# Soft-MoE dispatch softmax taken with a running maximum in two groups of chunks

## Chip, cores and metric

One core of a Trainium2 chip runs the whole program. The metric is device time in microseconds, the median of three runs. Engines are named as in the profile: PE is TensorE (PEld its weight loads), DVE VectorE, ACT ScalarE, POOL GpSimd, SP SyncE, whose queue issues nearly all transfers.

## What is computed

A two-dimensional Fourier transform of x (8 x 3072 x 256), of which the real part is kept, gives 24576 tokens of 256 numbers. A soft mixture of experts follows: 32 slots, dispatched by a softmax over all tokens, eight small experts, and a combining softmax over the slots. Then a feed-forward layer with a squared ReLU. Cut to what matters:

```python
X = np.fft.fft(np.fft.fft(x, axis=1), axis=2).real.reshape(24576, 256)
logits = X @ phi
d = np.exp(logits - logits.max(0, keepdims=True))
d /= d.sum(0, keepdims=True) + 1e-09
slot_input = d.T @ X
# experts: slot_out = relu(slot_input @ w1[e]) @ w2[e]
c = softmax of logits over the 32 slots
y = c @ slot_out
out = (s * np.maximum(y @ w_in, 0.0) ** 2 + b) @ w_out
```

The maximum in the third line runs over all 24576 tokens, one number for each of the 32 slots.

## The kernel before

The transform is never formed. phi is turned by the small transform along the 256 features first (phd), x is multiplied with it, and the long transform is done on 32 columns in place of 256. The stages, in the order of time:

- To about 90 us: x is read in 24 pages of 1 MiB, projected and partly transformed into `tt`.
- **Logits** (lines 553 to 611): 16 chunks `lp` of 112 partitions x 512, two at a time, each by eight small products. ScalarE copies a chunk to `lg` in SBUF, VectorE reduces it to 32 maxima in `cm` (L585). The two don't read one chunk at the same time: one is told to wait for the other. Behind the last chunk comes the maximum over all (L592), a transpose (L598), one reduction more (L603), a product that spreads the 32 numbers over all partitions (L607), and the copy `cmb`. Warm-up products of ones (`keep_warm`, L190) stand between on PE. Two VectorE steps of the preparation of w_out (L216, `side_step`) and six small ACT copies (`fill_stack`) lie in this gap too.
- **Transform of the exponentials** (L614 to L670, tiles `dt`, `hp`, `hh`): for each chunk the maximum is subtracted (POOL for odd chunks, DVE for even, L633), ACT takes the exponential (L669), PE makes four products with a table (`hp`, L652; the profile shows each as two), and ACT and DVE copy one half each to `hh` (L643). The four `dt` buffers are a pool of their own.
- **Sums** (L695 to L745, `htp`, `dps`, `racc`): `hh` is transposed, transformed once more and multiplied with the 24 pages `xrt` of x, which gives slot_input. Beside it DVE, POOL and ACT make the combining softmax (`c_steps`) and DVE prepares w_in and w_out (`side_step`, three steps in each round from the sixth on).
- **Experts** with w1 and w2, then the feed-forward part from about 232 us to the end.

The order on each engine is that in which the code is written; nothing reorders it. All large operands live in pages of 1 MiB (`page`, `drop`): 15 in `ring`, later some in smaller pools that take freed memory. The list `todo` holds the loads that are still to come in a fixed order: the 24 pages xrt, four pages of w_in among them, eight of w1, eight of w2. `pump()` issues the next as soon as the program has dropped a page, and SP waits at that load until the last reader of the page is done, with all later loads behind it.

Of the kernel before, what the change touches and what calls it, by code (L numbers as in the profile page):

```python
# [8 lines left out]
F32 = mybir.dt.float32  # L9
# [23 lines left out]
def tile_fft2__then__softmoe__then__act_relu2(  # L33
# [492 lines left out]
    cmb = keep.tile([P, NE], F32, name="cmb")  # L526
# [25 lines left out]
    temps = tc.alloc_tile_pool(name="temps", bufs=1, side="right")  # L552
    cm = temps.tile([R, NCH + 1, NE], F32, name="cm")
    cm1 = temps.tile([R, NE], F32, name="cm1")
    def lgf(i):
        return lg[i // 4][:, 4 * (i % 4):4 * (i % 4) + 4].rearrange("p k g e -> p (k g) e")

    with tc.tile_pool(name="ps_l", bufs=6, space=PSUM) as psl, \
            tc.tile_pool(name="ps_m", bufs=1, space=PSUM) as psm:
        mxp[:] = [psm, 1]  # L560
        done_l = 0
        for st in range(NCH // 2 + SKEW):
            halves = [(h, st - SKEW * h) for h in range(2) if 0 <= st - SKEW * h < NCH // 2]
            lps = {h: psl.tile([R, KC, NG * NE], F32, name="lp") for h, _ in halves}
            for k in range(2 * KC):
                q = P // 2 * (k % 2)
                m = M if q else P // 2
                for h, i8 in halves:
                    r = slice(64 * h, 64 * h + 64)
                    nc.tensor.matmul(  # L570
                        lps[h][q:q + m, k // 2, :], lhsT=ltabs[i8 // 4][0][r, 2 * KC * (i8 % 4) + k, 0:m],
                        rhs=tt[r, 2 * KC * i8 + k].rearrange("p b e -> p (b e)"), start=True, stop=True,
                        tile_position=(64 * h, q), skip_group_check=True,
                    )
            for h, i8 in halves:
                if h and i8 % 4 == 3:
                    drop(ltabs[i8 // 4][1])
                lp = lps[h]
                busy("dve", 0.55)
                at["pe"] += 1.06  # L580
                dst = lg[i8 // 2][:, 8 * (i8 % 2) + h:8 * (i8 % 2) + 8:2].rearrange("p k g e -> p k (g e)")
# [6 lines left out]
                if done_l == NCH - 4:  # L588
                    nc.vector.tensor_reduce(out=cm[:, NCH, :], in_=cm[:, :NCH - 4, :].rearrange("p i e -> p e i"), axis=AX.X,
                                            op=ALU.max)  # L590
                if done_l == NCH - 1:
                    nc.vector.tensor_reduce(out=cm1, in_=cm[:, NCH - 4:, :].rearrange("p i e -> p e i"), axis=AX.X,  # L592
                                            op=ALU.max)
                done_l += 1
        warm = psl.tile([R, 2, B * NE], F32, name="lp")[:, 0, :R]
        keep_warm(warm, 8)
# [3 lines left out]
        while side_step(0.0, True):  # L600
            pass
# [18 lines left out]
    def lgc(i):  # L620
        return lg[i // 4][:, 4 * (i % 4):4 * (i % 4) + 4]
# [688 lines left out]
```

## Time and profile before

| | |
|---|---|
| median of three runs | 1399.73 us (1397.64 to 1401.19) |
| span of the profiled execution | 1411.6 us |
| PE busy | 1388.2 us, 98% |
| DVE, ACT, POOL busy | 83%, 72%, 17% |
| chain that ended last, by engine | PE 88%, DMA 2%, DVE 1% |

The page gives the profiled execution's span and no other time of it. PE counts as busy while a product is in flight, so 98% does not say that it runs at its peak. The granted clock of PE has two levels, 2.4 GHz (shown as 1.00) and 1.2 GHz (0.50). The feed-forward part makes up five sixths of the span; the change lies in the stretch from 90 to 142 us.

### The profile page before, as it was taken

The page shows a single profiled execution, that of the slowest core. Times are in us where ns is not written, and L with a number is a line of the kernel's source. Part 1 is how long each engine was busy: PE and PEld are TensorE (multiplying, and loading weights), DVE is VectorE, ACT ScalarE, POOL GpSimd, SP SyncE. Part 2 cuts the span into 40 slices and gives each one's busy share as a digit, 9 for nine tenths or more (in the row PEclk, how much of TensorE's full clock was granted, in tenths as well). Part 3 has the DMA queues.
Part 4 walks back from the last instruction along what each step waited for, and adds up shares of the span by engine and source line. Part 5 has one row for each costly group of instructions (what it writes and reads, how often), then busy time and mean ns, then how long its engine had stood idle before and what let it go on. Part 6 is the DMA issues. An engine that isn't in the chain of part 4 may idle for free.

```text
span 1411.6 us, 23102 instructions
## 1 busy us (share of the span) xinstructions
PE 1388.2 (98%) x9036; PEld 856.0 (61%) x9036; DVE 1171.9 (83%) x1490; ACT 1010.7 (72%) x1423; POOL 233.1 (17%) x287
## 2 busy tenths in 40 slices
PE   8989999999999999999999999999999999999998
PEld 5669564566666666666666666666666666666665
DVE  1565764998989999999989898989898989888886
ACT  2774314877777777777877787877777777777775
POOL 1143400021212121211112121111111111111110
PEclk9995999999999999999999999999999999999999
DMA  8995795101010101101010101010101010101001
GB/s 352 414 311 229 291 414 225 29 27 36 20 36 23 36 24 29 30 23 32 23 36 21 34 23 36 23 33 23 36 23 36 23 36 23 33 23 36 23 20 30
DMA packets 72381, 112.27 MB, mean 80 GB/s; under 512 B 33904, under 2 KB 59632, under 8 KB 64976
## 3 DMA queue, kind: packets, MB, share of 16 engines
q1 hardware_dynamic: 72144, 110.70, 23.1%
q8 instruction: 71, 1.16, 0.3%
q14 instruction: 38, 0.31, 0.1%
q0 software_dynamic: 128, 0.10, 0.0%
HBM read 78.48 MB, written 25.17 MB: 73 GB/s over the span
## 4 chain that ended last, share of the span: by engine, by line
PE 88%; DMA 2%; DVE 1%; issue 1%; SPq 0%; ACT 0%; POOL 0%; DVEq 0%; ACTq 0%; POOLq 0%
PE op L1151 46%; PE op L1154 23%; PE fhp L1121 12%; PE racc L727 3%; DMA w2t<-in_moe_w_dram 2%; PE hp L652 2%; PE dps L712 1%; PE lp L570 1%; SPq L1084 0%; DVE cm L585 0%; DVE r L1127 0%; DVE rhl L1112 0%; PE eop L957 0%; DMA g<-gs 0%; PE gp L1055 0%
## 5 line engine op out<-in xcount | busy, mean ns | idle before, releaser
L1151 PE MATMUL op<-whl,rhl 128*128 128x512 f16 x3072 | 1025.3, 379 | 0.8 <-ACT rhl L1111 0.6
L1154 PE MATMUL op<-whl,rhl 128*128 128x256 f16 x3072 | 835.7, 273 | 0.0
L1126 ACT ACTIVATE r<-fhp,wsc 128x768 f32<-128x768 f32 (+1 forms) x513 | 461.8, 900 | 230.0 <-PE fhp L1121 228.8
L1127 DVE SCALAR_TENSOR_TENSOR r<-fhp,r 128x768 f32<-128x768 f32 (+1 forms) x513 | 488.9, 953 | 113.6 <-ACT r L1126 104.0
L1112 DVE TENSOR_TENSOR rhl<-r,rhl 128x768 f16<-128x768 f32 x511 | 506.9, 992 | 0.9 <-ACT rhl L1111 0.9
L1151 PEld LDWEIGHTS <-rhl 128*128 128x128 f16 x3072 | 300.5, 98 | 335.4 <-ACT rhl L1111 0.9
L1111 ACT CAST rhl<-r 128x768 f16<-128x768 f32 x511 | 420.1, 822 | 1.8 <-DVE r L1127 1.8
L1154 PEld LDWEIGHTS <-rhl 128*128 128x128 f16 x3072 | 300.6, 98 | 62.7 <-issue 0.3
L1166 POOL TENSOR_TENSOR ot<-ot,bias 128x256 f32<-128x256 f32 x189 | 138.1, 731 | 974.2 <-DVE ot L1164 974.2
L1121 PE MATMUL fhp<-ct,g 128*128 128x384 f16 x1024 | 250.4, 326 | 1.1 <-DMA g<-gs 0.8
L1121 PEld LDWEIGHTS <-g 128*128 128x128 f16 x1024 | 99.9, 98 | 69.0 <-issue 1.1
L1163 ACT ACTIVATE o<-op,small 128x256 f32<-128x256 f32 x189 | 90.0, 477 | 16.7 <-PE op L1154 16.7
L1164 DVE SCALAR_TENSOR_TENSOR ot<-op,small,o 128x256 f32<-128x256 f32 x192 | 91.7, 478 | 0.3
L394 PE MATMUL vt<-xb,phd 128*64 128x384 f32 (+3 forms) x288 | 49.0, 477 | 5.3 <-DMA xb<-in_x_turned_dram 5.3
L727 PE MATMUL racc<-xrt,dh 128*64 128x256 f32 x384 | 44.5, 383 | 0.4 <-DVE dh L717 0.4
L394 PEld LDWEIGHTS vt<-xb,phd 128*64 128x64 f32 x288 | 26.5, 139 | 25.5 <-issue 13.8
L727 PEld LDWEIGHTS racc<-xrt,dh 128*64 128x64 f32 x384 | 26.3, 137 | 20.9 <-issue 4.5
L419 DVE COPY v<-vq 128x512 f32<-128x512 f32 (+1 forms) x15 | 8.3, 593 | 33.9 <-PE vq L415 33.9
L406 ACT COPY vts<-vt 128x512 f32<-128x512 f32 (+1 forms) x16 | 8.5, 533 | 32.1 <-PE vt L394 32.0
L464 ACT COPY tt<-tps 32x512 f32<-32x512 f32 x48 | 27.7, 577 | 4.9 <-PE tps L450 4.4
L652 PE MATMUL hp<-htab_t,dt 112*128 112x104 f32 x128 | 27.6, 422 | 0.2 <-ACT dt L669 0.2
L652 PEld LDWEIGHTS hp<-htab_t,dt 112*128 112x128 f32 x128 | 27.4, 333 | 0.5 <-issue 0.5
(229 smaller groups left out, 518.0 us busy)
## 6 DMA issues: line engine op xcount, KB each, us to landing
xb<-in_x_turned_dram SPq DMA_DIRECT2D x24, 1024.0 KB, 20.1
xrt<-in_x_pages_dram SPq DMA_DIRECT2D x24, 1024.0 KB, 13.9
out_dram<-ot SPq DMA_DIRECT2D x128, 128.0 KB, 1.7
w1t<-in_moe_w_dram SPq DMA_DIRECT2D x8, 1024.0 KB, 13.7
out_dram<-ot SPq DMA_DIRECT2D x128, 64.0 KB, 2.0
raw<-in_moe_w_out_dram SPq DMA_DIRECT2D x4, 1024.0 KB, 20.3
raw<-in_moe_w_in_dram SPq DMA_DIRECT2D x4, 1024.0 KB, 7.8
w2t<-in_moe_w_dram SPq DMA_DIRECT2D x4, 1024.0 KB, 17.8
```

What stands on the lines that cost most here:

```text
L652: nc.tensor.matmul(hp[q][:, k, :], start=True, stop=True, lhsT=dt.rearrange("p k g e -> p (k g e)")[:, 128 * (2 * k + q):128 * (2 * k + q) ...
L727: nc.tensor.matmul(raccs[acc][64 * h:64 * h + 64, :], lhsT=dh[:, m, g].rearrange("p j e -> p (j e)"), rhs=xr[k][0][:, g, t, :], start=(sum ...
L1111: nc.scalar.copy(a, r2)
L1112: nc.vector.tensor_tensor(out=l, in0=r2, in1=a, op=ALU.subtract)
L1121: nc.tensor.matmul(hp[k * split][:, k, :].rearrange("p (s b m) -> p s b m", s=2, b=B), lhsT=g16[:, f * P:(f + 1) * P], rhs=c, start=True, ...
L1126: nc.scalar.activation(out=r[:, k], in_=hp[i][:, k], func=AF.Relu, scale=wsc[:, 2, p:p + 1])
L1127: nc.vector.scalar_tensor_tensor(out=r2[:, k], in0=hp[i][:, k], scalar=0.0, in1=r[:, k], op0=ALU.max, op1=ALU.mult)
L1151: nc.tensor.matmul(op.rearrange("p h d -> p (h d)"), lhsT=a, rhs=w.rearrange("p h d -> p (h d)"), start=(f == 0), stop=False)
L1154: nc.tensor.matmul(op[:, 0, :], lhsT=l, rhs=w[:, 0, :], start=False, stop=(f == NFC - 1))
L1163: nc.scalar.activation(out=o1, in_=op[:, 1, :], func=AF.Copy, scale=qv)
L1164: nc.vector.scalar_tensor_tensor(out=ot, in0=op[:, 0, :], scalar=qv, in1=o1, op0=ALU.mult, op1=ALU.add)
L1166: nc.gpsimd.tensor_tensor(out=ot, in0=ot, in1=bias, op=ALU.add)
```

## The change

The column maximum is taken in two groups. The first group (chunks of the first three of eight steps, six chunks) gets its maximum `cmb[0]` while the other logits are still being made (`top(0, ...)`); its chunks are subtracted from on POOL and DVE with that maximum. Their exponentials and transform stand directly behind the last logits on PE. The maximum of all 16 chunks, `cmb[1]`, is found between the first transform products (`top(1, ...)`) and used for the other ten. What the first group lacks is one factor for each slot, exp of the difference of the two maxima (`fac`), which POOL multiplies into the first group's part of `hh` in two passes (in place, 128 x 52 x 24 numbers each). The warm-up products are gone from here, DVE reduces a chunk before ACT copies it, two chunks share an `hp` tile and are copied at once, and of the copies of the first half of `hh` every third pair goes to DVE. `fill_stack` moves behind the fourth chunk. The scratch for the exponentials (seven buffers) and `cm` are two pages (`scr`) held from before the logits to the end of the transform. The steps of w_out that lay in the gap stay on the list of side work and are done among the sums.

```diff
-    cmb = keep.tile([P, NE], F32, name="cmb")
+    cmb = [keep.tile([P, NE], F32, name=f"cmb{g}") for g in range(2)]
...
+    GA, ND = 3, 7
+    scr = [page([R, 4, KC, NG, NE], F32, "scr") for _ in range(2)]
...
+    cm = scr[1][0][:, 3].rearrange("p k g e -> p (k g) e")
+    tmp = tabp.tile([P, 16, NE], F32, tag="tab", name="tmp")
+    cmr = [tmp[0:R, g] for g in range(2)]
+    dg = [tmp[0:NE, 2 + g] for g in range(2)]
+    cm2 = tmp[0:NE, 4]
+    dfa, fac = tmp[0:NE, 5, 0:1], tmp[:, 6, 0:1]
+    rep = tmp[0:NE, 8:12]
+    nc.gpsimd.tensor_copy(rep, ident[:NE, :NE].unsqueeze(1).to_broadcast([NE, 4, NE]))
...
+    def emit_d(i):
+        dts[i] = scr[i % ND // 4][0][:, i % ND % 4]
+        (nc.gpsimd if i in (0, 1, 2, 3) or i > 4 and i % 2 else nc.vector).tensor_tensor(
+            out=dts[i].rearrange("p k g e -> p (k g) e"), op=ALU.subtract, in0=lgc(i).rearrange("p k g e -> p (k g) e"),
+            in1=cmb[i >= 2 * GA][:R].unsqueeze(1).to_broadcast([R, 16, NE]),
+        )
+    def emit_exp(i):
+        for h in [slice(0, 2), slice(2, 4)] if i == 0 else [slice(0, 4)]:
+            nc.scalar.activation(out=dts[i][:, h], in_=dts[i][:, h], func=AF.Exp)
...
+    def top(g, step):
+        if step == 0:
+            nc.vector.tensor_reduce(out=cmr[g], in_=cm[:, 0:NCH if g else 2 * GA].rearrange("p i e -> p e i"), axis=AX.X, op=ALU.max)
+        elif step == 1:
+            top_t.append(psm.tile([P, P], F32, tag="tps", name="mt")[0:NE, 0:R])
+            nc.tensor.transpose(top_t[g], cmr[g], ident[:R, :R])
+        elif step == 2:
+            nc.vector.tensor_reduce(out=cm2[:, g:g + 1], in_=top_t[g], axis=AX.X, op=ALU.max)
+            nc.vector.tensor_scalar(out=dg[g], in0=ident[:NE, :NE], scalar1=cm2[:, g:g + 1], scalar2=None, op0=ALU.mult)
+        elif step == 3:
+            top_b.append(psm.tile([P, P], F32, tag="tps", name="mb")[:, 0:NE])
+            nc.tensor.matmul(top_b[g], lhsT=ones[:NE, :], rhs=dg[g], start=True, stop=True)
+        else:
+            nc.vector.tensor_copy(cmb[g], top_b[g])
+            if g:
+                nc.vector.tensor_tensor(out=dfa, in0=cm2[:, 0:1], in1=cm2[:, 1:2], op=ALU.subtract)
...
-                if done_l < NCH - 1:
-                    nc.scalar.copy(dst, lp)
-                lv = lp.rearrange("p k (b e) -> p (k b) e", e=NE)
-                nc.vector.tensor_reduce(out=cm[:, done_l, :], in_=lv.rearrange("p k e -> p e k"), axis=AX.X, op=ALU.max)
-                if done_l == NCH - 1:
-                    nc.scalar.copy(dst, lp)
...
-        warm = psl.tile([R, 2, B * NE], F32, name="lp")[:, 0, :R]
-        keep_warm(warm, 8)
-        mt = psm.tile([NE, R], F32, tag="mt", name="mt")
-        nc.tensor.transpose(mt, cm1, ident[:R, :R])
-        keep_warm(warm, 3)
-        while side_step(0.0, True):
-            pass
...
-        nc.vector.tensor_copy(cmb, mb)
-        mxp[0] = None
-        keep_warm(warm, 8)
-        fill_stack()
...
+        if st == GA + 1:
+            top(0, 1)
+        if st == GA + 2:
+            top(0, 3)
...
+            nc.vector.tensor_reduce(out=cm[:, 2 * i8 + h, :], in_=lv.rearrange("p k e -> p e k"), axis=AX.X, op=ALU.max)
+            nc.scalar.copy(dst, lp)
+            if n == 0 and st == GA + 1:
+                top(0, 2)
+            if n == 0 and st == GA + 2:
+                top(0, 4)
+        if st == GA:
+            top(0, 0)
+        if st == GA + 2:
+            for i in range(4):
+                emit_d(i)
+    top(1, 0)
+    emit_exp(0)
+    emit_exp(1)
+    emit_d(4)
+    emit_d(5)
...
+        def h_out(i, n):
+            o = 4 * (i % 2)
             for q in range(2):
-                hpv = hps[i][q].rearrange("p k (q c m) -> p (k q) c m", q=2, c=2)
-                eng = nc.vector.tensor_copy if q else nc.scalar.copy
-                eng(hh[q].rearrange("p m (c k) -> p k c m", c=2)[:, KC * i:KC * i + KC], hpv)
-            hps.pop(i)
+                hpv = hps[i // 2][q].rearrange("p k (q c m) -> p (k q) c m", q=2, c=2)[:, o:o + 4 * n]
+                eng = nc.vector.tensor_copy if q or (n > 1 and i // 2 % 3 == 2) else nc.scalar.copy
+                eng(hh[q].rearrange("p m (c k) -> p k c m", c=2)[:, KC * i:KC * (i + n)], hpv)
...
+            if i < 2:
+                top(1, 2 * i + 1)
+                top(1, 2 * i + 2)
+            if i == 3:
+                fp = psm.tile([P, P], F32, tag="tps", name="fp")[:, 0:1]
+                nc.tensor.matmul(fp, lhsT=rep.rearrange("p r e -> p (r e)"), rhs=dfa, start=True, stop=True)
...
+            if i > NCH - 2:
+                h_out(i - 1, 1)
+            elif i > 0 and i % 2 == 0:
+                h_out(i - 2, 2)
+            if 5 < i + 5 < NCH:
+                emit_d(i + 5)
...
+            if i + 2 < NCH:
+                emit_exp(i + 2)
+            if i == 3:
+                nc.scalar.activation(out=fac, in_=fp, func=AF.Exp)
+                fill_stack()
+            if i in (7, 11):
+                hq = hh[i // 11].rearrange("p m (c k) -> p m c k", c=2)[:, :, :, 0:2 * KC * GA]
+                nc.gpsimd.tensor_scalar(out=hq, in0=hq, scalar1=fac, scalar2=None, op0=ALU.mult)
+    for _, k_ in scr:
+        drop(k_)
```

PE behind the last logits, before: warm-up products (`L190`), the transpose `mt` and the spreading product `mb` stand ahead of the first `hp` product.

```order
L570 MATMUL lp<-tt,ltab 64x128
L570 MATMUL lp<-tt,ltab 48x128
L190 MATMUL lp<-ones 112x112 x8
L598 MATMUL mt<-ident,cm_785 32x112
L190 MATMUL lp<-ones 112x112 x3
L607 MATMUL mb<-dg,ones 128x32
L190 MATMUL lp<-ones 112x112 x8
L652 MATMUL hp_1038<-htab_t,dt 128x104
```

The same place in the change:

```order
L610 MATMUL lp<-tt,ltab 64x128
L610 MATMUL lp<-tt,ltab 48x128
L666 MATMUL hp_998<-htab_t,scr 128x104
L666 MATMUL hp_999<-htab_t,scr 128x104
L666 MATMUL hp_998<-htab_t,scr 128x104
L666 MATMUL hp_999<-htab_t,scr 128x104
L588 MATMUL mt<-ident,tmp 32x112
L666 MATMUL hp_998<-htab_t,scr 128x104
```

The transform's products follow the logits, and the second maximum's transpose stands among them.

DVE from the last logits on, before (`L585` reduces a chunk, `L589` and `L592` the reductions, `L216` is the side work):

```order
L585 TENSOR_REDUCE cm<-lp 112x32 x13
L589 TENSOR_REDUCE cm<-cm 112x32
L585 TENSOR_REDUCE cm<-lp 112x32 x3
L592 TENSOR_REDUCE cm_785<-cm 112x32
L216 SCALAR_TENSOR_TENSOR whl<-wo,wsc,whl 128x2x256 x2
L603 TENSOR_REDUCE cm_986<-mt 32x1
L605 TENSOR_SCALAR dg<-ident,cm_986 32x32
L608 COPY cmb<-mb 128x32
```

In the change:

```order
L627 TENSOR_REDUCE scr<-lp 112x32 x7
L585 TENSOR_REDUCE tmp<-scr 112x32
L627 TENSOR_REDUCE scr<-lp 112x32
L590 TENSOR_REDUCE tmp<-mt 32x1
L591 TENSOR_SCALAR tmp<-ident,tmp 32x32
L627 TENSOR_REDUCE scr<-lp 112x32 x2
L596 COPY cmb_757<-mb 128x32
L627 TENSOR_REDUCE scr<-lp 112x32 x6
L585 TENSOR_REDUCE tmp<-scr 112x32
```

The first group's three short steps have moved in among the chunk reductions, `L589` and the side work are gone from here, and only the second group's reduction is left behind the last chunk.

SP around the end of the transform, before, with what each load waits for (a load of one of the 24 xrt pages; DMAHW is the landing of the eighth load before it, the engines are the readers of the page):

```order
L326 DMA xrt_1224<-in_x_pages_dram 128x2048 [waits DVE_49,DMAHW2_49,Activation_49,Pool_49]
L326 DMA xrt_1226<-in_x_pages_dram 128x2048 [waits DMAHW3_49,PE_49,Pool_49]
L326 DMA xrt_1228<-in_x_pages_dram 128x2048 [waits DMAHW4_49,PE_49,Pool_49]
L326 DMA xrt_1275<-in_x_pages_dram 128x2048 [waits DMAHW5_49,PE_49]
L326 DMA xrt_1324<-in_x_pages_dram 128x2048 [waits DMAHW6_49,PE_49]
```

In the change:

```order
L326 DMA xrt_1079<-in_x_pages_dram 128x2048 [waits DMAHW0_49,PE_49,Pool_49]
L326 DMA xrt_1159<-in_x_pages_dram 128x2048 [waits DMAHW1_49,PE_49,Pool_49]
L326 DMA xrt_1161<-in_x_pages_dram 128x2048 [waits DMAHW2_49,DVE_49,Activation_49]
L326 DMA xrt_1163<-in_x_pages_dram 128x2048 [waits DMAHW3_49,DVE_49,Activation_49]
L326 DMA xrt_1210<-in_x_pages_dram 128x2048 [waits DMAHW4_49,PE_49]
```

The second and third rows before wait for the two halves of the table `htab`, freed in the middle and at the end of the transform, and the fourth for the first sum: one load starts at the end of the stage. In the change the first row waits for the first half of the table; the next three for its second half and for the two scratch pages, all freed at the end of the stage; the last for the first sum. Ten of the 24 pages xrt stand ahead of the stage's end there, against thirteen.

## Rows read from the trace of the kernel before

**Rows 1.** Timeline of PE: start us, us, line, instruction, idle before it.
```profile
98.89 6.72 PE L570 MATMUL lp<-tt,ltab 64*48 64x128 f32 x132 [3.88 <-issue]
105.54 1.82 PE L190 MATMUL lp<-ones 128*112 128x112 f32 x16
108.61 0.27 PE L598 MATMUL mt<-ident,cm 112*32 112x112 f32 x1 [1.25 <-DVE cm L592]
...
110.44 0.63 PE L607 MATMUL mb<-dg,ones 32*128 32x32 f32 x2 [0.97 <-DVE dg L605]
```

**Rows 2.** Chain that ended last, in order of time: start us, us, what.
```profile
105.58 0.73 DVE cm L589
106.31 1.80 DVE cm L585 x3
108.14 0.42 DVE cm L592
108.56 1.32 DVE whl L216 x2
...
111.45 1.72 POOL dt L633
...
114.55 27.61 PE hp L652 x128
...
203.89 18.57 DMA w2t<-in_moe_w_dram
222.48 9.61 DMA w2t<-in_moe_w_dram
```

**Rows 3.** Table by stretch; its first row names the columns.
```profile
core 0: us, PE busy (x) PEld busy (x) DVE busy (x) ACT busy (x) POOL busy (x), PEclk, DMA share, GB/s
...
93.20:96.50 3.30, 1.64 (x46) 1.16 (x36) 3.30 (x6) 2.22 (x5) 2.98 (x5) 1.00 1.06 235
...
103.40:106.80 3.40, 3.40 (x66) 3.00 (x59) 3.08 (x5) 2.05 (x4) 0.00 (x0) 1.00 1.01 419
106.80:110.20 3.40, 1.43 (x13) 1.07 (x11) 3.26 (x8) 1.46 (x7) 0.00 (x0) 1.00 1.02 417
110.30:114.50 4.20, 3.89 (x18) 3.56 (x18) 2.65 (x4) 1.90 (x4) 3.05 (x2) 0.50 1.02 421
114.50:142.20 27.70, 27.65 (x130) 27.67 (x131) 10.96 (x22) 13.96 (x29) 7.97 (x7) 0.50 0.40 161
...
155.00:203.90 48.90, 48.90 (x397) 27.93 (x396) 37.24 (x49) 7.01 (x13) 5.91 (x6) 1.00 0.99 396
...
142.20:155.00 12.80, 12.15 (x105) 7.28 (x104) 10.22 (x21) 6.11 (x11) 8.74 (x9) 0.92 0.53 176
```

**Rows 4.** Timeline of ACT, where the logits resume.
```profile
100.36 1.07 ACT L583 COPY lg<-lp 112x512 f32<-112x512 f32 x2 [4.94 <-PE lp L570]
```

**Rows 5.** Instructions on tile lp: ns min/median/max, first and last start us.
```profile
L585 DVE TENSOR_REDUCE cm<-lp x16: 680/681/693, 92.2 to 107.4; 112x32 f32<-112x512 f32 x16
L583 ACT COPY lg<-lp x15: 586/591/632, 91.6 to 105.1; 112x512 f32<-112x512 f32 x15
```

**Rows 6.** Groups by line, 114 to 142.3 us: busy us, mean ns, idle before.
```profile
L633 POOL TENSOR_TENSOR dt<-lg,cmb 112x512 f32<-112x512 f32 x7 | 9.3, 1336 | 14.6 <-ACT hh L643 14.6
L669 ACT ACTIVATE dt<-dt 112x512 f32<-112x512 f32 x14 | 8.8, 627 | 0.0
L643 DVE COPY hh<-hp 128x208 f32<-128x208 f32 x16 | 8.4, 522 | 17.5 <-PE hp L652 17.5
L643 ACT COPY hh<-hp 128x208 f32<-128x208 f32 x16 | 8.2, 514 | 13.5 <-PE hp L652 13.5
```

**Rows 7.** Groups by line on POOL, 89 to 95 us, the same columns.
```profile
L513 POOL COPY ltab<-ltab 64x2048 f32<-64x2048 f32 x1 | 1.9, 1895 | 0.9 <-DMA ltab<-in_ltab_dram 0.9
```

**Rows 8.** Transfers, 142 to 235 us: queue, packets, MB, share of 16 engines.
```profile
q1 hardware_dynamic: 6352, 32.51, 88.8%
```

More of the change, by code (lines that the diff above doesn't have):

```diff
@@ new lines, in tile_fft2__then__softmoe__then__act_relu2 @@
+    top_t, top_b = [], []
+    psl = tc.alloc_tile_pool(name="ps_l", bufs=6, space=PSUM)
+    for st in range(NCH // 2 + SKEW):
+        halves = [(h, st - SKEW * h) for h in range(2) if 0 <= st - SKEW * h < NCH // 2]
+        lps = {h: psl.tile([R, KC, NG * NE], F32, name="lp") for h, _ in halves}
+        for k in range(2 * KC):
+            q = P // 2 * (k % 2)
+            m = M if q else P // 2
+            for h, i8 in halves:
+                r = slice(64 * h, 64 * h + 64)
+                nc.tensor.matmul(
+                    lps[h][q:q + m, k // 2, :], lhsT=ltabs[i8 // 4][0][r, 2 * KC * (i8 % 4) + k, 0:m],
+                    rhs=tt[r, 2 * KC * i8 + k].rearrange("p b e -> p (b e)"), start=True, stop=True,
+                    tile_position=(64 * h, q), skip_group_check=True,
+                )
+        if st == GA + 1:
+            top(0, 1)
+        if st == GA + 2:
+            top(0, 3)
+        for n, (h, i8) in enumerate(halves):
+            if h and i8 % 4 == 3:
+                drop(ltabs[i8 // 4][1])
+            lp = lps[h]
+            busy("dve", 0.55)
+            at["pe"] += 1.06
+            dst = lg[i8 // 2][:, 8 * (i8 % 2) + h:8 * (i8 % 2) + 8:2].rearrange("p k g e -> p k (g e)")
+            lv = lp.rearrange("p k (b e) -> p (k b) e", e=NE)
+            nc.vector.tensor_reduce(out=cm[:, 2 * i8 + h, :], in_=lv.rearrange("p k e -> p e k"), axis=AX.X, op=ALU.max)
[9 more added lines that the diff above has]
+                emit_d(i)
@@ L617, in tile_fft2__then__softmoe__then__act_relu2 @@
     hh = [(hpool if q else hpool0).tile([P, 2 * MH, P], F32, name=f"hh{q}") for q in range(2)]
[L618 to L621 removed]
     pst = tc.alloc_tile_pool(name="ps_t", bufs=2, space=PSUM)
[L624 to L639 removed]
+    with tc.tile_pool(name="ps_h", bufs=2, space=PSUM) as psh:
+        def h_out(i, n):
+            o = 4 * (i % 2)
@@ L646, in tile_fft2__then__softmoe__then__act_relu2 @@
+                eng(hh[q].rearrange("p m (c k) -> p k c m", c=2)[:, KC * i:KC * (i + n)], hpv)
         hps = {}
-        for i in range(-3, NCH + 1):
-            if 0 <= i < NCH:
+        for i in range(NCH + 1):
+            if i < NCH:
                 dt = dts.pop(i)
-                hp = [psh.tile([P, 2, 8 * MH], F32, name=f"hp{q}") for q in range(2)]
+                if i % 2 == 0:
+                    hps[i // 2] = [psh.tile([P, 4, 8 * MH], F32, name=f"hp{q}") for q in range(2)]
+                hp = hps[i // 2]
@@ L651, in tile_fft2__then__softmoe__then__act_relu2 @@
                 for k, q in [(0, 0), (1, 0), (0, 1), (1, 1)] if i == NCH - 1 else [(0, 0), (0, 1), (1, 0), (1, 1)]:
                     nc.tensor.matmul(
[L653 removed]
+                        hp[q][:, 2 * (i % 2) + k, :], start=True, stop=True,
                         lhsT=dt.rearrange("p k g e -> p (k g e)")[:, 128 * (2 * k + q):128 * (2 * k + q) + 128],
```

74 lines of the change are left out of this document (7 added, 67 removed).

## The prediction

> **What bounds the kernel now.** I read the chain of waits first. Two of its pieces matter here. From 105.6 to 114.55 us it runs through the column maximum: VectorE reductions, a transpose, and the first subtraction on GpSimd, while TensorE has nothing but warm-up products to do [rows 1, 2]. Then 27.61 us of transform products in one piece [rows 2]. The second piece is 203.89 to 232.1, the w2 transfers, behind which the feed-forward part starts [rows 2]. Nothing in the diff touches that part, so the end moves by as much as the landing of the last w2 load moves, no more.
>
> Next the table by stretch. It shows two things that the chain hides. The granted clock falls to 0.50 (1.2 GHz) for the stretch that begins at 110.3 and stays there through the whole transform stage, although TensorE is busy in 27.65 of its 27.7 us [rows 3]. At 1.2 GHz TensorE is the bound of that stage: ScalarE is busy 13.96 and VectorE 10.96 of 27.7. And the transfers: share 1.02 to 114.5, but 0.53 between 142.2 and 155, then 0.99 to 203.9 [rows 3]. So from about 155 on the end is set by how much is still to be loaded and how early the queue fills, and both hang on the end of the transform stage, because the page that each load needs is freed by the sums that follow it.
>
> **Start of the transform.** The last logits product ends at 105.6 (98.89 + 6.72) [rows 1]. Before, VectorE had a partial reduction of 0.73 in the way and finished the last three chunks at 108.1 (106.31 + 1.80) [rows 2]. In the changed kernel that reduction is gone; in its place stand, between the last nine chunk reductions, three short steps of the first group's maximum, each no longer than the 0.42 of the final reduction [rows 2], together some 0.7. TensorE has the pair of chunks that it resumes at 98.89 ready at about 100.4, where ScalarE's copy begins [rows 4]; nine reductions at 0.65 (0.68 each [rows 5], overlapping a little) and 0.7 from there give 107.0, with the waits between 107.3. Then one ScalarE copy, 0.59 [rows 5], now behind the reduction instead of ahead of it, and half an exponential: between half of and the whole 0.63 [rows 6], I take 0.4. First transform product at about 108.4, against 114.55: **-6.1 us**. If VectorE is as late as before, 108.1, it is 109.2 and -5.3; if it waits for nothing, -6.5. The four subtractions of the first group are on GpSimd, 1.34 each [rows 6], from about 103.3, behind four of the nine reductions and the short steps: the first is done by 104.6, the fourth by 108.7, and TensorE at 1.72 per chunk (27.61/16) wants the fourth at 113.6. They are hidden, with 5 us to spare.
>
> **Length of the stage.** The same 128 products and loads. If the clock is 1.2 GHz all along, 27.6. Added in the stream: the second group's transpose, its spreading product and the product for the correction factor. The trace has the first two at 0.27 and 0.63 [rows 1]; the third is of the second's kind. Bounds 0 (if they hide) and 1.5; I take **+0.8**, since loads and products alternate without overlap at this clock (27.67 and 27.65 busy of 27.7 [rows 3] at 0.216 a pair). The clock can still be at 2.4 GHz for the first two chunks: each then takes half of its 1.72, which is worth up to 1.7 less the wait for the second exponential, so 0 to 1.5; I take **-0.7**. Everything else that the stage gains or loses lies beside TensorE: merged copies to hh, 0.51 to 1.03 each for two chunks instead of 2 x 0.51 [rows 6], the six copies of fill_stack, ten subtractions on GpSimd instead of eight. ScalarE's work adds up to some 17 us (worked out under the first rival), and VectorE's is less. The two correction passes over hh on GpSimd are new: 1248 numbers each. GpSimd's rows go from 0.92 ns a number (1895 ns for 2048 [rows 7]) to 2.6 (1336 ns for 512 [rows 6]), so 1.2 to 3.3 us; I take 3. The first stands ahead of the subtractions of chunks 13 and 15: it can start at about 119.6, when chunks 4 and 5 are copied, and chunk 13 is wanted at 131.6, so it costs nothing up to about 8 us. End of the stage: 142.2 - 6.1 + 0.8 - 0.7, about 136.2: **-6.0**.
>
> **Pages.** Two pages now hold scratch from the logits to the end of the stage, and one page of w_out weights is kept longer, since its two last VectorE steps (1.32 [rows 2]) move from the gap into the sums. Read off the order, 34 MiB instead of 31 are still to be loaded when the stage ends; three loads start at once instead of one. Behind the stage 32.51 MB went through the queue [rows 8], which is 31 MiB. Full rate is 417 to 421 GB/s [rows 3], 2.5 us for 1 MiB: 3 x 2.5 = 7.5 us more transfer. Against it, 142.2 to 155 has 0.47 x 12.8 = 6.0 us of idle queue and 155 to 203.9 has 0.01 x 48.9 = 0.5 [rows 3], and three loads in hand fill just that idle time. Bounds 0 (a gain is out, since more is loaded) and +7.5; I take 7.5 - 6.5 and 0.2 for the hole that the fifth load leaves, which still waits for a sum: **+1.2**. The sums themselves don't wait: they use 24 pages in the 61.7 us from 142.2 to 203.9, so the ten that are in hand last some 26 us.
>
> Sum: -6.0 + 1.2 = **-4.8 us**. The profiled span is 1411.6, 11.9 above the median of the three runs, 1399.73; what lies between is not shown, so I take the difference off the median: 1394.9.
>
> **Rivals.** (1) *The clock holds.* The pause of TensorE is then 105.6 to 108.4 and the warm-up products are gone. If the chip grants 2.4 GHz through the stage, products take 27.6/2 = 13.8 and ScalarE becomes the bound: 16 exponentials at 0.63, five merged copies at 0.9, two single ones, and about 1.6 for the factor and fill_stack (seven short instructions, taken at half of a copy's 0.51 or less), 17.2 in all [rows 6], from 107.9 to 125.1, against 142.2. That is -17.1 + 1.2, or 1383.8; if the clock falls half-way, around 1390. For it: from 103.4 to 110.2 the clock was 1.00 [rows 3], so the stage would be entered with it. Against it: it fell behind 93.2 to 96.5, where TensorE was busy 1.64 of 3.3, and again behind 106.8 to 110.2 with 1.43 of 3.4 [rows 3], and the transform's products alone never brought it back in 27.7 us. The new kernel's first microseconds look like those stretches. The Trainium skill (TensorE: Matmul & The Clock Gate, section Why this matters for your kernels) ties a lost clock to an idle pause between bursts; by that rule this short pause would keep 2.4 GHz and the time would be this rival's. The trace speaks against it: behind 106.8 the longest pause was 1.25 us [rows 1], and the clock was lost.
>
> (2) *No net gain.* The three loads find no idle time, because the releases behind the first sums stay what they were: -6.0 + 7.5, or 1401.2, inside the bound of no change. For it: the loads from the fourth on wait for the same sums. Against it: they wait with three in hand instead of one.
>
> (3) *Slower: the load queue stands still.* SyncE issues in order. The thirteenth load behind the stage now waits for the moved w_out step on VectorE, which stands behind that engine's softmax steps. With thirteen loads in hand the queue runs dry some 33 us behind the stage's end; from there each microsecond of lateness is a microsecond of the whole. On top of rival 2, 3.7 us late gives 1405. For it: VectorE is the fullest engine after TensorE there, 37.24 of 48.9 [rows 3]. Against it: I place the step some 25 us behind the stage's end, 8 us early.
>
> **How the numbers follow.** A difference of 0.3%, 4.2 us, is what a measurement of this kernel can tell from no change. Chances: forecast 0.60 (1390.5 to 1398.5, from -5.3 or -6.5 at the start, 0 to +1.5 for the inserted products, 0 to -1.5 for the clock, 0 to +4 for the pages); rival 1 0.18; rival 2 0.13; rival 3 0.09. Of the forecast's own 0.60 somewhat over half lies below 1395.5, say 0.34. Faster 0.34 + 0.18 = 0.52, same 0.26 + 0.13 = 0.39 less 0.01 of rival 2 that ends slower, slower 0.10. The range takes the forecast, the upper part of rival 2 and most of rival 1: 1383.5 to 1401.5.
>
> **What would show it.** In the profile after: first transform product 6 us earlier than 114.55; the clock at 0.50 and the stage near 28 us long (forecast) or at 1.00 and some 17 us long (rival 1); the transfer share behind the stage near 1.0 at once (forecast), as low as 0.53 again (rival 2), or a hole some 35 us later with SyncE waiting for L216 (rival 3). The last w2 load should land 4 to 6 us earlier than 232. If the stage ends 6 us earlier and that landing doesn't move, the term of the pages is wrong; if the stage is short, the clock is.

## The result

The changed kernel is slower: 1412.35 us, median of four executions (1410.71 to 1417.21), against 1400.46 us for the kernel before, a ratio of 1.0091 with a 95% interval of 1.0069 to 1.0114. The forecast was 1394.9 us, faster; 1412.35 lies above its range.

The two profiles seem to say the opposite. The changed kernel's span is 1410.4 us, that of the kernel before 1411.6. Wherever an execution is listed with both numbers its time is its span plus 1.7 to 2.1 us (1412.23 and 1410.4 for the profiled execution after). So the profiled execution of the kernel before must have taken about 1413.4 us (1411.6 and some 1.8), while its timed ones took 1397.64 to 1403.55. The profile of before was not one of its usual executions. The list of cores of both kernels (span, mean granted clock) gives the first hint why (the usual executions of before, listed below, have 0.993 or more); the first line is of before, the second of after:

```profile
core 0: 1411.6 us, clock 0.984
...
```
```profile
core 0: 1410.4 us, clock 0.987
...
```

### The profile page after: what moved, and what is told of

It is laid out like the page before. It is cut to its first block, busy times and chain, and to the rows that moved or that the text cites. A ratio compares the mean times of both kernels' runs of the same rounds, so it can differ in the third digit from the quotient of the medians.

```text
span 1410.4 us, 23022 instructions
## 1 busy us (share of the span) xinstructions
PE 1383.7 (98%) x9003; PEld 850.5 (60%) x9003; DVE 1171.5 (83%) x1487; ACT 1009.5 (72%) x1415; POOL 243.4 (17%) x292
## 4 chain that ended last, share of the span: by engine, by line
PE 90%; DMA 8%; DVE 1%; SPq 0%; issue 0%; ACT 0%; POOL 0%; DVEq 0%; ACTq 0%; POOLq 0%
PE op L1178 46%; PE op L1181 23%; PE fhp L1148 12%; DMA xb<-in_x_turned_dram 4%; PE racc L753 3%; DMA w2t<-in_moe_w_dram 2%; PE hp L666 2%; DMA ltab<-in_ltab_dram 2%; PE dps L738 1%; PE vt L394 1%; PE lp L610 1%; DVE r L1154 0%; SPq L1111 0%; DVE rhl L1139 0%; PE tps L450 0%
## 5 line engine op out<-in xcount | busy, mean ns | idle before, releaser
L1191 DVE SCALAR_TENSOR_TENSOR ot<-op,small,o 128x256 f32<-128x256 f32 x192 | 91.6, 478 | 0.3
L394 PEld LDWEIGHTS vt<-xb,phd 128*64 128x64 f32 x288 | 26.8, 139 | 25.6 <-issue 12.9
L464 ACT COPY tt<-tps 32x512 f32<-32x512 f32 x48 | 27.7, 577 | 4.9 <-PE tps L450 4.4
L666 PE MATMUL hp<-htab_t,scr 112*128 112x104 f32 x128 | 27.2, 411 | 1.7 <-ACT scr L577 1.7
L666 PEld LDWEIGHTS hp<-htab_t,scr 112*128 112x128 f32 x128 | 26.5, 320 | 2.1 <-ACT scr L577 2.0
## 6 DMA issues: line engine op xcount, KB each, us to landing
raw<-in_moe_w_in_dram SPq DMA_DIRECT2D x4, 1024.0 KB, 11.9
```

The costliest lines, as they stand in the source:

```text
L394: nc.tensor.matmul(vt[64 * h:64 * h + 64, o:o + k, :], lhsT=phd[:, c, sg, :], rhs=turned(pg, c, i, k, rev), start=(c == 0 and m < 2), stop ...
L1191: nc.vector.scalar_tensor_tensor(out=ot, in0=op[:, 0, :], scalar=qv, in1=o1, op0=ALU.mult, op1=ALU.add)
```

## The profile after

Timeline of PE in the changed kernel (start us, us, line, instruction, idle before it), in place of [rows 1]:

```profile
106.75 0.64 PE L610 MATMUL lp<-tt,ltab 64*64 64x128 f32 x7 [1.17 <-issue]
109.10 1.14 PE L666 MATMUL hp<-htab_t,scr 112*128 112x104 f32 x8 [1.72 <-ACT scr L577]
...
112.27 3.74 PE L666 MATMUL hp<-htab_t,scr 112*128 112x104 f32 x16
116.45 20.81 PE L666 MATMUL hp<-htab_t,scr 112*128 112x104 f32 x96
137.36 1.11 PE L730 MATMUL htp__1166<-ident,hh 128*128 128x128 f32 x4
```

The first transform product starts at 109.10 in place of 114.55. TensorE pauses 1.72 us ahead of it. The transform ends at 137.26 (116.45 + 20.81), 4.9 us earlier than the 142.16 of before, and takes 28.16 us against 27.61 [rows 2].

The chain that ended last (start us, us, what), in place of [rows 2]:

```profile
107.42 0.70 DVE scr L627
108.17 0.46 issue
108.63 0.43 ACT scr L577
109.10 1.14 PE hp L666 x8
...
200.30 20.39 DMA w2t<-in_moe_w_dram
220.70 9.62 DMA w2t<-in_moe_w_dram
```

Between the last logits and the transform only a reduction, a copy (under "issue" here) and half an exponential are left. But the last w2 load lands at 230.32, only 1.8 us earlier than the 232.09 of before.

The table by stretch, with the columns of [rows 3]:

```profile
103.70:107.10 3.40, 2.23 (x67) 1.99 (x56) 3.00 (x6) 3.21 (x6) 3.15 (x3) 1.00 1.01 417
107.10:110.40 3.30, 1.58 (x17) 1.33 (x13) 2.94 (x3) 2.48 (x7) 3.03 (x3) 1.00 1.02 432
110.50:137.30 26.80, 26.76 (x123) 26.05 (x121) 11.78 (x20) 12.68 (x27) 14.87 (x8) 0.50 0.32 126
137.40:150.20 12.80, 12.27 (x100) 7.30 (x102) 9.73 (x21) 6.11 (x11) 8.03 (x8) 0.85 0.86 331
```

The clock was still 1.00 in the stretch in which TensorE paused (busy 1.58 of 3.3 us), fell to 0.50 at 110.5, 1.4 us into the transform, and stayed there to the end of it. Behind it the transfers have a share of 0.86, where they had 0.53 [rows 3]. The start, the clock, the length of the stage and this share are what the forecast wanted to see; the landing, which was to come 4 to 6 us earlier, and the time are not.

## Experiments

**Theory A**: in its usual executions the kernel before keeps 2.4 GHz through the transform, because warm-up products fill the gap ahead of it. The change took them out and so pays half speed there every time. **Theory B**: the 12 us are lost elsewhere, in the later loads or the side work.

### The kernel before, once more

No edit. 

> The kernel before, unchanged. Theory A (the clock): in its usual execution the granted clock stays at 1.00 through the transform, the stage is some 10 us shorter than the 27.7 us of the profile shown, and the execution takes about 1400 us; the profile shown, whose span of 1411.6 us lies 11.9 above the median, was one that lost the clock at 110.2. So a new profile at about 1400 us should show 1.00 from 114 to 127 and no 0.50, and most timed executions a mean clock above the 0.984 of the profile shown; one near 1412 would show 0.50 again. Theory B (the difference lies elsewhere, for instance in the transfers or the side work of the later stages): a new profile at about 1400 us shows 0.50 through the transform and 27 to 28 us for it as before, and the 12 us are missing somewhere behind 145 us.

Measured: 1399.39 us, median of 12, mean clocks 0.993 to 0.999. Timeline of PE (first fence) and table by stretch (second) of this profile, whose span is 1399.3 us:

```profile
107.33 0.43 PE L570 MATMUL lp<-tt,ltab 64*64 64x128 f32 x4 [1.47 <-issue]
107.69 2.31 PE L190 MATMUL lp<-ones 128*112 128x112 f32 x16
...
111.85 3.33 PE L190 MATMUL lp<-ones 128*112 128x112 f32 x16
115.39 14.72 PE L652 MATMUL hp<-htab_t,dt 112*128 112x104 f32 x128 [0.21 <-ACT dt L669]
```
```profile
105.50:108.80 3.30, 1.83 (x23) 1.42 (x19) 3.30 (x6) 0.83 (x2) 0.00 (x0) 1.00 1.03 425
108.90:112.20 3.30, 3.30 (x18) 2.95 (x17) 2.40 (x8) 1.46 (x7) 0.00 (x0) 0.50 1.04 427
112.30:115.60 3.30, 3.08 (x17) 2.85 (x16) 2.25 (x2) 1.90 (x4) 3.30 (x2) 0.50 1.03 427
115.70:130.10 14.40, 14.40 (x128) 14.24 (x127) 10.44 (x21) 13.22 (x29) 7.67 (x6) 1.00 0.89 368
```

The same 128 products take 14.72 us, not 27.61. Even here the clock fell in the gap, at 108.9, but warm-up products went on until 115.2, it came back at 115.7, and the transform kept it. In the first profile of before the same products ran at the same place, and the clock did not come back:

```profile
111.01 3.33 PE L190 MATMUL lp<-ones 128*112 128x112 f32 x16
```

In the runs of this study the kernel before was executed 104 times: 101 times with a mean clock of 0.993 or more in 1393.6 to 1406.0 us, and three times with 0.984 to 0.986 in 1412.4, 1412.9 and 1414.6 us. An execution of the first kind is said below to keep the clock, one of the second (0.988 or less) to lose it. The profile that the prediction stands on is of the second kind.

### The kernel before without its warm-up products

```diff
-        keep_warm(warm, 8)
         mt = psm.tile([NE, R], F32, tag="mt", name="mt")
         nc.tensor.transpose(mt, cm1, ident[:R, :R])
-        keep_warm(warm, 3)
...
-        keep_warm(warm, 8)
```

> The kernel before without the 19 warm-up products (8, 3 and 8) between the last logits product and the first transform product; nothing else is changed. Theory A: the clock falls to 0.50 in that gap in every execution, the transform takes 27 to 28 us, and the time is 1410 to 1414 us, 0.7 to 1.0% above the kernel before. Theory B: the products do nothing that lasts, and the time is 1398 to 1402 us.

Measured: 1414.61 us, ratio 1.0098 (1.0068 to 1.0128), all six executions at a mean clock of 0.984 to 0.986; 0.6 above the range of theory A and far from that of B. Taking out the 19 products alone cost 14.7 us, more than the 11.9 that the change lost. Its timeline of PE shows what they also cost:

```profile
113.52 27.61 PE L648 MATMUL hp<-htab_t,dt 112*128 112x104 f32 x128 [1.50 <-ACT dt L665]
```

From the end of the last chunk's reduction on VectorE to this product are 4.47 us (109.05 to 113.52). With warm-up products it was 6.45 in the first profile of before (108.10 to 114.55) and 6.44 in the second (108.95 to 115.39), and the changed kernel has 0.99 (108.11 to 109.10). So of the 5.5 us that the start gained, 2.0 were the warm-up products, most of them at half speed, and 3.5 the reordering.

### The changed kernel with warm-up products in the gap

```diff
+    warm = psl.tile([R, 2, B * NE], F32, name="lp")[:, 0, :R]
+    keep_warm(warm, 8)
     top(1, 0)
     emit_exp(0)
```

> The changed kernel with 8 warm-up products between its last logits product and its first transform product, where TensorE paused 1.7 us. Theory A: if these are enough, the clock stays at 1.00, the stage takes 17 to 19 us in place of 28, and the time is 1395 to 1402 us; if they are not, the clock falls again at about 110 and the time is 1410 to 1414. Theory B: 1411 to 1414 us whatever the clock does, since the 12 us are lost elsewhere.

Measured: 1399.68 us, ratio 1.0006 (0.9980 to 1.0032); 11 of 12 executions at a mean clock of 0.995 or more, one at 0.986 with 1415.45 us. Timeline of PE and table by stretch:

```profile
108.54 1.82 PE L190 MATMUL lp<-ones 128*112 128x112 f32 x16
110.78 1.14 PE L668 MATMUL hp<-htab_t,scr 112*128 112x104 f32 x8 [0.41 <-ACT scr L577]
...
118.33 5.83 PE L668 MATMUL hp<-htab_t,scr 112*128 112x104 f32 x50 [0.72 <-ACT scr L577]
124.38 3.93 PE L668 MATMUL hp<-htab_t,scr 112*128 112x104 f32 x30 [0.22 <-DVE hh L658]
```
```profile
108.90:112.20 3.30, 2.89 (x28) 2.71 (x28) 2.97 (x5) 3.28 (x8) 3.30 (x3) 1.00 1.03 434
110.80:128.30 17.50, 16.39 (x133) 15.39 (x133) 14.67 (x20) 13.74 (x30) 16.40 (x10) 1.00 0.55 219
```

Eight products in a pause that was idle anyway win back the whole 12 us. Theory A holds and B falls. A second question comes up: at 2.4 GHz on both sides the transform starts 0.99 us behind the last reduction instead of 6.44, yet the time is that of the kernel before. Part of the answer stands in the fence: the stage takes 17.53 us (110.78 to 128.31) against 14.72, and GpSimd is busy 16.40 of 17.5.

### More and fewer warm-up products

With 4 in the gap instead of 8: 

> The changed kernel with 4 warm-up products in the gap instead of 8 (with 8, 11 of 12 executions kept the clock). Theory A in its plain form (any product in the gap will do): most executions stay at a mean clock of 0.994 or more and take 1397 to 1402 us. Theory A in its graded form (the clock falls the more often the less is issued in the gap): executions of both kinds, some at 0.984 to 0.987 and 1411 to 1416 us, more than 1 of 12.

Measured: 1400.30 us, ratio 1.0002 (0.9976 to 1.0028); again 11 of 12 kept the clock (0.994 or more), one lost it (0.983, 1414.15 us). Four are not told apart from eight.

With 16 more behind the first four chunks:

```diff
+            if i < 4:
+                keep_warm(warm2, 4)
             if i < 2:
                 top(1, 2 * i + 1)
```

> As the run before it, with 4 more warm-up products behind each of the first four chunks of the transform, 16 in all. Theory A: the clock stays at 1.00 in most executions, the stage takes 18 to 20 us, the time is 1393 to 1402 us. Theory B: 1412 to 1416 us, since the products only add 3 to 4 us of TensorE's time at the most.

Measured: 1402.69 us, ratio 1.0017 (0.9998 to 1.0036), just above the range expected. All 12 executions stayed at 0.995 or more, and the time is 3.0 us above that with 8 products in the gap; the 16 in the stage take 3.8 (0.96 behind each of the four chunks). A high mean does not say that the clock never fell. The table by stretch of this profile:

```profile
107.80:111.00 3.20, 1.72 (x25) 1.29 (x19) 2.17 (x4) 2.29 (x4) 3.20 (x4) 1.00 0.99 412
111.20:114.40 3.20, 3.10 (x16) 2.86 (x16) 2.20 (x3) 2.76 (x6) 1.69 (x2) 0.50 1.00 422
114.60:133.80 19.20, 18.44 (x161) 17.73 (x159) 12.93 (x18) 11.93 (x26) 13.83 (x8) 1.00 0.43 175
```

The clock fell here while the eight products of the gap ran, as in the second profile of before, and was back in the transform's first chunk. So the products let the stage run at 2.4 GHz; they do not always keep the clock from falling ahead of it. Over all seven runs of the changed kernel with such products (12 executions each), 4 of 84 lost the clock; without them, 8 of 8 did.

### The change at half speed on both sides

The changed kernel, unchanged, and beside it the kernel before without warm-up products. 

> The changed kernel, unchanged. Theory A: it has no product between its last logits product and its first transform product, so it loses the clock in nearly every execution: mean clock 0.981 to 0.988 and 1410 to 1414 us in at least 10 of 12. At equal clock it is to be compared with the kernel before without its warm-up products, run beside it: the predicted gain of the reordering itself was 4.8 us. By the two profiles at 0.50, counted from the last product ahead of the logits, it is between 0 and 2 us.

> The kernel before without its 19 warm-up products, once more, beside the changed kernel. Theory A: mean clock 0.984 to 0.987, 1413.5 to 1415.5 us, none near 1400. If the reordering itself gave the 4.8 us predicted, the changed kernel beside it would take 1409 to 1410.5; if it gives 0 to 2, 1412 to 1414.5.

Measured: 1412.08 us, ratio 1.0088 (1.0067 to 1.0110), clocks 0.985 to 0.987; and 1412.10 us, ratio 1.0097 (1.0076 to 1.0119), clocks 0.984 to 0.987, four executions each. Together with the first pair (1412.35 and 1414.61, not run beside each other) the medians put the reordering by itself between 0 and 2.3 us at half speed; with four to six executions on a side and up to 7 us between them this is no exact number, but the 4.8 predicted was not seen. The 1412.10 lies below the 1413.5 to 1415.5 expected of it. Timeline of PE of the changed kernel in this run:

```profile
108.48 2.04 PE L666 MATMUL hp<-htab_t,scr 112*128 112x104 f32 x8 [2.33 <-ACT scr L577]
...
117.08 20.81 PE L666 MATMUL hp<-htab_t,scr 112*128 112x104 f32 x96
```

Its pause was 2.33 us, the clock was at 0.50 from the first product on, and the stage took 29.41 us (108.48 to 137.89) against the 28.16 of the first profile, whose first 1.4 us were at 1.00.

### The pages alone

The kernel before without warm-up products, its transform scratch in two pages:

```diff
+    scr = [page([R, 4, KC, NG, NE], F32, "scr") for _ in range(2)]
...
-            dts[i] = temps.tile([R, KC, NG, NE], F32, tag="dt", name="dt", bufs=4)
+            dts[i] = scr[i % ND // 4][0][:, i % ND % 4]
```

> The kernel before without warm-up products, so at 0.50 through the transform (1414.6 us measured for that), and with the scratch of the transform in two pages that are held from the logits to the end of the stage, instead of in a pool of its own; nothing else of the change. Theory R (the pages cost what the two profiles differ by): the last of the w2 loads lands 2 to 3 us later behind the stage's end than without them, and the time is 1416.5 to 1418 us. As predicted for the pages: +1.2, so 1415.8 us. Rival (the pages cost nothing, the difference comes from elsewhere in the change): 1414 to 1415 us.

Measured: 1413.96 us, ratio 1.0099 (1.0085 to 1.0114), within the 1412.10 and 1414.61 without pages. The rival holds: two held pages cost nothing that shows. The edit also gives seven scratch buffers in place of four; the transform takes 27.61 us as without them. The tables by stretch, from the end of the transform to the landing of the last w2 load, tell why. The columns are those of [rows 3]; the last two numbers count. In this order: the kernel before (the first profile), the same without warm-up products (its first run), this run, the changed kernel, and at 2.4 GHz the kernel before and the changed kernel with 8 warm-up products:

```profile
142.20:232.10 89.90, 88.40 (x784) 50.22 (x782) 52.81 (x86) 20.82 (x33) 15.79 (x16) 0.99 0.92 363
```
```profile
141.10:232.80 91.70, 89.69 (x785) 50.26 (x783) 52.84 (x86) 20.83 (x33) 15.78 (x16) 0.98 0.91 356
```
```profile
140.70:232.30 91.60, 88.33 (x784) 49.66 (x782) 52.56 (x86) 20.78 (x33) 15.77 (x16) 0.99 0.96 379
```
```profile
137.30:230.30 93.00, 89.44 (x784) 50.98 (x784) 53.43 (x89) 20.77 (x34) 15.82 (x16) 0.98 0.96 385
```
```profile
130.10:219.80 89.70, 87.79 (x785) 49.23 (x784) 52.70 (x86) 20.94 (x34) 15.77 (x16) 1.00 0.92 364
```
```profile
128.30:219.70 91.40, 89.07 (x785) 50.67 (x784) 53.38 (x89) 21.24 (x35) 16.83 (x17) 0.98 0.97 392
```

Rate times length is 31.1 MiB for the three profiles of the kernel before without pages, 33.1 with the two pages, and 34.2 for the changed kernel at either clock. The idle part of the queue, one less the share, is 7.2 us, 8.3, 3.7, 3.7, 7.2 and 2.7. So the held pages do move 2 to 3 MiB behind the stage, and these fill 3.5 to 4.6 us of idle queue there. Between this run and the kernel without pages the way to the last landing is the same (91.6 and 91.7 us). The changed kernel's 93.0 and 91.4 lie above the 89.9 and 89.7 of before, but the kernel before itself varies by 1.8 us from profile to profile, so that difference isn't clear.

What is idle less behind the stage is idle more within it. At 2.4 GHz the stage's rows, both shown above, have a share of 0.89 over 14.4 us in the kernel before and of 0.55 over 17.5 in the changed kernel with 8 products: 1.6 us of idle queue and 7.9. Stage and way to the landing together make 8.8 us for before and 10.6 for the change.

### Is GpSimd the bound of the stage?

The changed kernel with 8 warm-up products and without its two passes over `hh` (`hq`, the multiplication with the factor is left out). 

> The changed kernel with 8 warm-up products in the gap and without the two GpSimd passes that multiply the first group's columns by the factor: that multiplication is left out altogether. Theory P: without the 7.4 us of passes no subtraction waits behind one, the stage takes 15 to 15.8 us in place of 17.5, and the time is 1396.5 to 1398.5 us against 1399.7 with them. Rival (ScalarE is the bound, with 16 exponentials and its copies): the stage stays at 17 us or more and the time at 1399 to 1400.

Measured: 1399.06 us, ratio 1.0007 (0.9987 to 1.0028). Two of the twelve executions lost the clock (1413.67 and 1417.01 us); the ten that kept it have a median of 1398.4, against 1399.4 for the eleven with the passes, which is not clear of noise. The stage took 16.57 us (109.54 to 126.11), 0.96 less than with the passes, which is neither theory's number. The passes are a third of the 2.8 us. VectorE's subtractions are slower too. Groups by line of the changed kernel (first fence, 108 to 138 us, clock 0.50), with warm-up products (second, 110 to 129 us, clock 1.00) and without the passes (third, 109 to 127 us), shape, count, busy us, mean ns, idle before:

```profile
L695 POOL TENSOR_SCALAR hh<-hh,tmp 128x1248 f32<-128x1248 f32 x2 | 7.4, 3712 | 1.3 <-ACT scr L577 1.3
...
L570 DVE TENSOR_TENSOR scr<-lg,cmb 112x512 f32<-112x512 f32 x6 | 5.7, 947 | 0.1
```
```profile
L570 DVE TENSOR_TENSOR scr<-lg,cmb 112x512 f32<-112x512 f32 x6 | 7.1, 1177 | 0.0
```
```profile
L570 DVE TENSOR_TENSOR scr<-lg,cmb 112x512 f32<-112x512 f32 x6 | 5.1, 843 | 0.1
```

The same subtraction took 0.68 us in the second profile of before, and 1.16 in the version below, which has no passes either: how much of its slowness is due to the passes stays open, and so does the rest of it. The rest of the 2.8 us are the three products put into the stream (0.26, 0.40 and 0.38 at this clock) and chunks for which the exponential isn't ready (0.72 at 118.33).

### A version without the passes

10 warm-up products, the factor applied in the copies, of which the first wait for it, a third pair of `hp` buffers, `fill_stack` in the logits:

```diff
...
+                if i >= 2 * GA:
+                    (nc.vector.tensor_copy if dv else nc.scalar.copy)(hv, hpv)
+                elif dv:
+                    nc.vector.tensor_scalar(out=hv, in0=hpv, scalar1=fac, scalar2=None, op0=ALU.mult)
+                else:
+                    nc.scalar.activation(out=hv, in_=hpv, func=AF.Copy, scale=fac)
...
-            if i in (7, 11):
...
-                nc.gpsimd.tensor_scalar(out=hq, in0=hq, scalar1=fac, scalar2=None, op0=ALU.mult)
```

> The changed kernel with 10 warm-up products in the gap, the factor of the first group applied inside the copies of chunks 0 to 5 instead of by two GpSimd passes of 3.4 to 4.0 us, a third pair of transform buffers so that the first copies can wait for it, and the six small ScalarE copies of the constants moved into the logits. Theory P (with the clock at 1.00 the stage is bound by GpSimd, whose passes stand between its subtractions): the stage takes 14.5 to 15.5 us in place of 17.5, ends 4 to 5 us earlier than that of the kernel before at the same clock, and the time is 1395 to 1397.5 us. Theory Q (the loads behind the stage set the end whatever the stage gains): the stage gets shorter all the same, the time stays at 1399 to 1400 us.

> The version with 10 warm-up products and the factor in the copies, once more, to narrow its interval. By the profiles its transform starts 5.3 us earlier behind the last column maximum than in the kernel before and takes 16.4 us in place of 14.7, which leaves 3.7 us at the end of the stage. If that reaches the end, the time is 3 to 4 us below the kernel before, a ratio of 0.997 to 0.998; if the loads behind the stage swallow it, the ratio is 0.999 to 1.001, as in the first run of it (0.9991).

Measured: 1398.75 us, ratio 0.9991 (0.9969 to 1.0012), and in the second run 1399.19 us, ratio 0.9993 (0.9979 to 1.0006); none of the 24 executions lost the clock. Timeline of PE and chain of the second run:

```profile
110.67 1.11 PE L674 MATMUL hp<-htab_t,scr 112*128 112x104 f32 x8
...
117.81 9.18 PE L674 MATMUL hp<-htab_t,scr 112*128 112x104 f32 x80 [0.49 <-ACT scr L577]
128.03 0.63 PE L736 MATMUL htp__1175<-ident,hh 128*128 128x128 f32 x4 [1.04 <-DVE hh L660]
```
```profile
189.59 18.97 DMA w2t<-in_moe_w_dram
208.57 10.72 DMA w2t<-in_moe_w_dram
```

The stage took 16.36 and 16.32 us in the two runs, not the 14.5 to 15.5 of theory P. In the second run the transform ends at 126.99, 3.1 us earlier than in the second profile of before; the last w2 load lands at 219.29 against 219.84 there (210.22 + 9.62). The gain is given back between the two (92.3 us in place of 89.7), as theory Q has it, and everything after hangs on that landing. The version is not told apart from the kernel before, whose own second run came out at a ratio of 0.9992.

The same with one page of scratch instead of two: 

> The version with the factor in the copies and 10 warm-up products, with the scratch of the transform in one page instead of two: the column maxima and three of the seven scratch buffers lie in pools of their own that end with the logits and the stage. One load more may start while the transform runs. Theory R (held pages cost transfer time, which sets the end): the last w2 load lands some 2.5 us earlier, and the time is 1395.5 to 1396.5 us against 1398.75 with two pages. Rival (the idle time behind the stage takes the load anyway, as the run with the scratch of the kernel before in two pages suggests): 1398 to 1399.5 us.

Measured: 1400.24 us, ratio 1.0008 (0.9995 to 1.0022). Tables by stretch, of the stage and from its end to the last landing, with two pages (the second run above) and with one:

```profile
110.70:127.00 16.30, 15.80 (x133) 15.21 (x133) 13.78 (x19) 12.24 (x23) 7.51 (x5) 1.00 0.56 218
127.00:219.30 92.30, 88.32 (x784) 50.05 (x784) 53.38 (x89) 21.19 (x35) 15.78 (x16) 1.00 0.96 388
```
```profile
109.70:126.00 16.30, 15.82 (x133) 15.22 (x133) 14.20 (x19) 12.25 (x23) 7.72 (x6) 1.00 0.74 302
126.00:219.30 93.30, 88.32 (x785) 50.00 (x784) 53.38 (x89) 21.19 (x35) 15.76 (x16) 1.00 0.93 372
```

Nothing gained: 33.1 MiB follow the stage instead of 34.2, and the queue is idle 4.2 us in the stage instead of 7.2, but 6.5 behind it instead of 3.7. The sum, 10.7 against 10.9, is what it was. The rival holds here too.

## Why the prediction was wrong

**The base of the difference** is the step that failed. "The profiled span is 1411.6, 11.9 above the median of the three runs, 1399.73; what lies between is not shown, so I take the difference off the median." A span can't be longer than the time of its own execution, so nothing lay between; the profile was of an execution slower than the median by some 13.7 us. The row that explained it was on the page, [rows 3] with the clock at 0.50 for 27.7 us, and the text read it as a property of the kernel ("stays there through the whole transform stage"). The stage takes 27.61 us there and 14.72 in a usual execution, 12.9 of the 13.7. Taken off that execution's own 1413.4, the forecast's -4.8 gives 1408.6, and 1412.35 was measured: of the miss of 17.5 us the base is 13.7.

**Costing the warm-up products at nothing** is the same error from the other side. The text called their gap one in which TensorE has "nothing but warm-up products to do" and let them go for free. The cover that they gave was the clock of the next 14.7 us, worth 12.1 to 14.7 us (the two runs without them, against the kernel before beside each).

**The clock in the changed kernel** was forecast rightly: 0.50 in both of its profiles, with stages of 28.16 and 29.41 us, and a mean of 0.981 to 0.988 in all eight executions. Rival 1's stage at 2.4 GHz came near too: 17.2 worked out, 17.53 measured once the products were put back. That is in part luck, since ScalarE, the bound of that sum, was busy only 13.74 of the 17.5 us and TensorE 16.39. But the rival gave 1383.8 for it, since it subtracted from a median in which the clock was held already. In weighing it the prediction named the Trainium skill (TensorE: Matmul & The Clock Gate, section Why this matters for your kernels), whose rule ties a lost clock to an idle pause between bursts, and set [rows 1] against that rule. By that rule the pause was too short to lose the clock. The trace and the runs disagree: pauses of 1.72 and 2.33 us in the two profiles, the first with TensorE busy 1.58 of 3.3, and the clock lost in 8 executions of 8. They agree with the page's advice as such, since filling the pause kept it 80 times of 84.

**Start**: -6.1 forecast, -5.45 measured. VectorE was done with the last chunk at 108.11, not 107.3; from there to the first product took 0.99, with 1.0 assumed. The text's own figure for a late VectorE, -5.3, came within 0.15 us.

**Length of the stage**: +0.1 forecast, +0.55 measured at half speed, and +1.8 in the second profile of the changed kernel. That one ran at 0.50 from its first product on, so the products put into the stream cost 1.8 us, above the bound of 1.5, and the 1.00 at the start of the first profile gave back 1.25 where 0.7 was taken. The reading behind the +0.8 was wrong as well: loads and products that are busy 27.67 and 27.65 of the same 27.7 us lie over each other, they do not alternate. The passes on GpSimd take 3.7 us each, above the bound of 3.3, and hide at this clock. At 2.4 GHz, where the comparison should have been made, the stage is 2.8 us longer than before.

**Pages**: +1.2 forecast, +3.1 between the two profiles. The parts were right: 34 MiB in place of 31 (34.2 and 31.1), three loads at once, the transfer share 0.86 behind the stage. The idle queue took 3.5 us of the 7.5 in the profile after, not 6.5. Of the pairs at equal clock the one at 2.4 GHz (first profile with products, second of before) gives +1.7, within what the same kernel varies by, and the pages alone gave nothing. The term left out the stage itself, where the held pages leave the queue idle for longer.

**Rival 3** didn't come: no hole behind the stage, and the share is 1.01 from 160 to 200 us. The slower side came by no rival named, but by the clock that the change took away.

Put together at 2.4 GHz on both sides: -5.45 at the start, +2.8 in the stage, +1.7 behind it is -1 us, and 1399.68 against 1399.96 was measured. That the reordering gains nothing measurable is shown; that it gains exactly 1 is not. A slip of adding stands in the forecast's own bounds: put together, its parts give 1391.7 to 1399.9, not 1390.5 to 1398.5. It changes nothing in the outcome.

## What to carry to other kernels

Put the profiled execution's time beside the timed ones before a row of it is used; if the span is longer than the median, ask first which row belongs to that execution alone. Warm-up products have no consumer, and a chain of waits shows at most the time that they take: what they cover is the clock of the work behind them, and whoever takes them out has to cost that work at both clocks. Where a stage's end releases transfers that set the end of the whole, count the queue's idle time in the stage and behind it together: here a shorter stage moved that time and did not lessen it.

## What was not expected of the hardware

The transform's own products keep the clock, but by themselves they did not bring it back in any profile. Once at 1.00 they ran at 1.00 for 14.4 us with TensorE busy all of it; at 0.50 they stayed there for 27 us with TensorE busy 26.76 of 26.8, and so to the end of the stage in all six profiles of that kind. Where it came back between the last logits and the end of the transform (at 115.7 in the second profile of before, at 114.5 in that with 16 more products), warm-up products stood ahead of them. That these are enough is not shown: in the first profile of before the same products did not bring it back. And the same program with the same products kept or lost it from one execution to the next, 101 to 3 in the kernel before. The Trainium skill (TensorE: Matmul & The Clock Gate, section What's actually happening) says that the point at which the clock changes differs between runs of one kernel. The two profiles of before agree: the clock fell 4.7 us behind the last logits product in the first (110.3 and 105.6) and 1.1 us in the second (108.9 and 107.8).
